# Fused FFT convolution and Mish MLP on one Trainium2 core: h's octet transform moved directly in front of kv's

## The chip, the cores and the metric

The kernel runs on one core of a Trainium2 chip. A core has five engines with a queue of their own each: TensorE (PE, matrix products, with its weight loads listed as PEld), VectorE (DVE), ScalarE (ACT), GpSimd (POOL) and SyncE (SP, which here only issues DMAs). Each engine works its queue off in order, and an instruction that waits for another engine's count (a semaphore) holds up all that stands behind it. Products land in PSUM, from where ScalarE or VectorE must copy them out. The metric is the device time of one execution in microseconds; lower is better.

## The reference, cut to what matters

With S = 2048 positions, D = 448 channels, F = 1792:

```python
xn = _layernorm(A_q)
# A: an H3 block
k_shift = sum_t k_pad[:, t:t + S, :] * shift_k[:, ks - 1 - t]     # causal, 4 taps
kv = k_shift * v
y = irfft(rfft(kv, 2 * S) * rfft(ssm_k, 2 * S))[:, :S] + kv * ssm_D
A = xn * y
# B: an MLP
h = xn @ w1 + b1
B = (h * tanh(softplus(h))) @ w2
return A_q + A + B
```

All of it is float32. The long convolution is done by a transform in stages, written as small matrix products.

## The kernel before, in words

The MLP is the spine. It is cut into 8 chunks of 256 positions (`NCHUNK`), and each chunk into 7 pairs of 128 columns of F (`NP`), 56 pairs in all. A pair takes two **slots** (half steps) on TensorE: an even slot with its first product (`g1_mm`, line 494, 22 matrix products), an odd slot with the Mish of this pair on ScalarE (`mish`, line 502, with a cast `ach` and on VectorE the remainder `acl`, line 81) and the second product of the pair two before (`g2_mm`, lines 519 to 521, 12 products). Float32 is made of a high and a low part, so each product is done three times.

The convolution is laid between these slots by a plan of numbers: `at(slot, fn)` puts a piece ahead of the slot's MLP work, `after(slot, fn)` behind it. First come the transforms over 64 points (`f1_mm`, for the filter "h" and for "kv"); their results go to DRAM. From slot 63 on come eight **octets** o. For each:

- `o_load` (lines 195 to 201): SyncE loads the octet's part of h's and of kv's first transform, tiles "ah" and "av" (one buffer each), and the matrices "g"; `gi_load` loads "gi" for the way back.
- `h2_mm` and `v2_mm` (line 214): the second transform, 16 products each into two PSUM tiles "pc". The trace lists each as two instructions, so a block is 32. They use a quarter of the array each, 64 rows by 32 columns.
- `h2_out` and `v2_out` (lines 225 and 234): the copies from PSUM to the tiles "hs" and "vs".
- `prod` (line 247): the complex product of the two on VectorE, in two parts of three instructions: part 0 makes "ya" (with "yb"), part 1 "yc" (with "yd"). The four tiles have one buffer each.
- `i1_mm` (line 257): the first step of the way back, from "ya" and "yc" into two tiles "pc"; `i1_out` (line 265) copies them out and stores them to the DRAM tile "E".

The pool "pc" has two tiles in all, of two PSUM banks each. Octet o has its kv block in slot s = 65 + 3 o and its inverse in slot s + 4, one slot after the kv block of octet o + 1. So three slots hold, in turn, kv of o, the inverse of o - 1, and h of o + 1. Between these VectorE also normalises the inputs of chunks 5 to 7 (`nt_norm`, line 434, tiles "xn", and `nt_split`, line 442, "XL"), takes their statistics (line 389), and adds the MLP's result (`g2_evac`, line 526, tile "qt"). Small VectorE pieces are put between the larger ones by `dv()`.

After the octets, from slot 98, the last step of the way back follows (`i2_mm`, `gate`), and then the end of the MLP.

Of the kernel before, what the change touches and what calls it, by code (L numbers as in the profile page):

```python
# [14 lines left out]
S, D, F = 2048, 448, 1792  # L15
# [13 lines left out]
H0_AT = 63  # L29
# [10 lines left out]
def tile_kernel(ctx: ExitStack, tc, q, qT, k, v, sk, hT, sD, w10, w1, b1, w2, c_f1, c_id, c_g, c_gi, c_i2, out):  # L40
    nc = tc.nc
    V = nc.vector
# [14 lines left out]
    Dh = dp.tile([NO * 16, 32, D], F32, name="Dh")  # L57
# [39 lines left out]
    def at(slot, fn, *args):  # L97
        plan.setdefault(int(slot), []).append((fn, args))

    def after(slot, fn, *args):  # L100
        plan2.setdefault(int(slot), []).append((fn, args))
# [85 lines left out]
    GT, AH, AV, HS, PV, Y = {}, {}, {}, {}, {}, {}  # L187

    def t2(shape, name, bufs=1):
        if not sp2:  # L190
            ph1.close()
            sp2.append(ph2.enter_context(tc.tile_pool(name="ph2", bufs=1, reuse_waits="tile")))
        return sp2[0].tile(shape, F32, name=name, bufs=bufs)
# [28 lines left out]
    def h2_out(o):  # L222
        HS[o] = t2([128, 2, 2, D], "hs", 2)
        for c, p in enumerate(PS.pop(("H", o))):
            nc.scalar.copy(HS[o][:, c], p[:, :, :D])  # L225

    def v2_mm(o):
        PS["V", o] = [f2_mm(AV[o], o, c) for c in range(2)]
# [353 lines left out]
    for g, t in enumerate(KV_AT):  # L582
        d = t - (KV_AT[g - 1] if g else t - 6)
# [17 lines left out]

    for o in range(NO):
        s, d = OCT_AT[0] + OCT_AT[1] * o, OCT_AT[1]
        h = s - 1 if o else H0_AT
        (at if o else after)(h - d if o else h - 4, o_load, AH, Dh, o, "ah")
        at(s - d if o else s - 2, o_load, AV, Dkv, o, "av")
        at(h, h2_mm, o)
        after(h, h2_out, o)
        at(s, v2_mm, o)
        after(s, v2_out, o)  # L610
        at(s, gi_load, o)
        after(s + 1, prod, o, 0)
        after(s + 2, prod, o, 1)
        at(s + 4, i1_mm, o)
        after(s + 4, i1_out, o)

# [84 lines left out]
    for s in range(nslots):  # L701
        j = s // 2 - G2_LAG - 1
        if s % 2 == 0 and j >= 0 and pairs[j][1] == NP - 1:
            g2_evac(pairs[j][0])
        for fn, args in plan.pop(s, ()):
            fn(*args)
        mlp_slot(s)
        fns = plan2.pop(s, ())
        for fn, args in fns:
            if fn in (h2_out, v2_out, i1_out):  # L710
                fn(*args)
        for fn, args in fns:
            if fn not in (h2_out, v2_out, i1_out):
                fn(*args)
# [66 lines left out]
```

## Time and profile before

| | |
|---|---|
| median of 3 runs | 365.48 us (365.23 to 365.75) |
| profiled execution, its time | 365.54 us |
| its span | 363.8 us |
| mean granted clock of TensorE | 0.998 |
| busy: TensorE, VectorE, ScalarE | 98%, 74%, 46% of the span |
| the octets (h of octet 0 to the inverse of octet 7) | 182.0 to 293.5 us of the span |

The span is the time between the first and the last instruction of the profile; the rest of the execution's time lies around it. In the timeline a row gives start, duration, engine, line, operation, tiles (out<-in) and, in brackets, the idle time ahead of it and what ended it. In the chain of work a row gives start, duration, engine, tile and line.

### The profile page before, as it was taken

Reading aid. Unit: us, or ns where it says so; the run is one execution under the profiler, and the core shown is the slowest. Engines: PE = TensorE matmul, PEld = TensorE weight load, DVE = VectorE, ACT = ScalarE, POOL = GpSimd, SP = SyncE. Lnnn points to the kernel's source line nnn. Section 1 sums busy time; section 2 is a strip of 40 time slices with the busy share of each in tenths; the row PEclk is TensorE's granted clock in tenths of the full one; section 3 lists DMA queues with packets and bytes.
Section 4 is the critical chain, followed back from the end, with each engine's and each line's share of the span. In section 5 each row is a group of like instructions: output and inputs, shape, how many; then the busy total and the mean of one; then the engine's idle time right before and its main releaser. Section 6 shows DMA issues by size and latency. Waiting matters only on the chain.

```text
span 363.8 us, 7474 instructions
## 1 busy us (share of the span) xinstructions
PE 357.8 (98%) x3110; PEld 290.1 (80%) x3110; DVE 267.4 (74%) x367; ACT 166.4 (46%) x279; POOL 74.3 (20%) x67
## 2 busy tenths in 40 slices
PE   8999999999999999999999999999999999999995
PEld 2988888888888989988967666666666889889885
DVE  5798658999998988797427755767665734997741
ACT  4866552344333433343255555547655534225450
POOL 3027002931028223604000020000010005112020
PEclk9999999999999999999999999999999999999999
DMA  7999978758686438525877798898898486959656
GB/s 251 353 270 349 413 300 231 225 158 264 154 264 199 92 121 268 146 70 119 235 261 217 258 245 218 290 272 219 266 271 189 90 253 235 406 221 278 108 68 135
DMA packets 32515, 81.69 MB, mean 225 GB/s; under 512 B 3025, under 2 KB 19026, under 8 KB 32482
## 3 DMA queue, kind: packets, MB, share of 16 engines
q1 hardware_dynamic: 21266, 47.16, 39.1%
q10 hardware_dynamic: 8240, 19.34, 21.6%
q0 software_dynamic: 2976, 14.73, 13.8%
q8 instruction: 24, 0.39, 0.4%
q14 instruction: 9, 0.07, 0.1%
HBM read 52.77 MB, written 28.45 MB: 223 GB/s over the span
## 4 chain that ended last, share of the span: by engine, by line
PE 54%; DVE 2%; ACT 1%; ACTq 1%; issue 0%
PE pg L494 20%; PE pg L519 7%; PE pc L214 7%; PE pg L521 7%; PE pg L520 7%; PE pc L257 4%; PE pc L314 2%; ACTq L268 1%; DVE x L178 1%; PE pc L131 1%; DVE x L181 0%; ACT qe L265 0%; ACT a L502 0%; ACT hs L225 0%; DVE qt L526 0%
## 5 line engine op out<-in xcount | busy, mean ns | idle before, releaser
L502 ACT ACTIVATE a<-pg,b1t 128x256 f32<-128x256 f32 x112 | 47.2, 473 | 109.1 <-PE pg L494 95.8
L494 PE MATMUL pg<-XH,w1h 128*128 128x256 f32 x448 | 90.8, 285 | 0.4 <-DVE XL L457 0.2
L494 PEld LDWEIGHTS pg<-XH,w1h 128*128 128x128 f32 x448 | 69.7, 188 | 18.7 <-issue 16.5
L519 PE MATMUL pg<-w2h,ach 128*128 128x448 f32 x224 | 83.2, 371 | 0.0
L520 PE MATMUL pg<-w2l,ach 128*128 128x448 f32 x224 | 81.3, 363 | 0.2 <-DVE w2l L81 0.2
L521 PE MATMUL pg<-w2h,acl 128*128 128x448 f32 x224 | 81.4, 363 | 0.0
L81 DVE TENSOR_TENSOR acl<-a,ach 128x512 fp32r<-128x512 f32 x56 | 38.7, 691 | 57.5 <-ACT ach L80 57.4
L494 PE MATMUL pg<-XL,w1h 128*128 128x256 f32 x448 | 69.7, 277 | 0.0
L494 PEld LDWEIGHTS pg<-XL,w1h 128*128 128x128 f32 x448 | 59.5, 188 | 0.0
L494 PE MATMUL pg<-XH,w1l 128*128 128x256 f32 x336 | 56.8, 278 | 0.0
L519 PEld LDWEIGHTS pg<-w2h,ach 128*128 128x128 f32 x224 | 42.0, 187 | 14.4 <-issue 12.2
L494 PEld LDWEIGHTS pg<-XH,w1l 128*128 128x128 f32 x336 | 46.9, 188 | 0.0
L520 PEld LDWEIGHTS pg<-w2l,ach 128*128 128x128 f32 x224 | 42.1, 188 | 2.8 <-DVE w2l L81 0.5
L521 PEld LDWEIGHTS pg<-w2h,acl 128*128 128x128 f32 x224 | 42.1, 188 | 2.6
L80 ACT CAST ach<-a 128x512 fp32r<-128x512 f32 x56 | 34.7, 620 | 1.8
L161 POOL TENSOR_TENSOR x<-kr,skb 128x896 f32<-128x896 f32 x8 | 17.0, 2126 | 74.5 <-DVE x L160 53.2
L178 DVE TENSOR_TENSOR x<-x 128x896 f32<-128x896 f32 x24 | 26.3, 1097 | 2.7 <-POOL x L161 2.2
L398 POOL TENSOR_TENSOR mv<-ve,mhalf 128x2 f32<-128x2 f32 x3 | 3.7, 1248 | 97.9 <-DVE ve L395 97.9
L402 POOL TENSOR_SCALAR xn<-qt,mv,rstd 128x448 f32<-128x448 f32 x8 | 21.8, 2720 | 0.4
L137 ACT COPY st<-pc 128x896 f32<-128x896 f32 x16 | 14.5, 906 | 14.5 <-PE pc L131 12.6
L138 DVE TENSOR_TENSOR st<-pc,st 128x896 f32<-128x896 f32 x16 | 17.4, 1088 | 4.5 <-ACT st L137 4.1
L265 ACT COPY qe<-pc 128x896 f32<-128x896 f32 x16 | 13.8, 911 | 12.0 <-PE pc L257 11.8
(85 smaller groups left out, 404.1 us busy)
## 6 DMA issues: line engine op xcount, KB each, us to landing
Dkv<-st ACTq DMA_DIRECT2D x16, 448.0 KB, 6.2
ah<-Dh SPq DMA_DIRECT2D x8, 896.0 KB, 7.4
av<-Dkv SPq DMA_DIRECT2D x8, 896.0 KB, 6.3
E<-qe ACTq DMA_DIRECT2D x16, 448.0 KB, 5.7
e<-E POOLq DMA_DIRECT2D x8, 896.0 KB, 8.0
kr<-in_k_dram SPq DMA_DIRECT2D x10, 448.0 KB, 6.5
Dh<-st ACTq DMA_DIRECT2D x10, 448.0 KB, 5.7
x<-in_hT_dram SPq DMA_DIRECT2D x8, 448.0 KB, 6.9
```

The source lines that it names most:

```text
L80: nc.scalar.copy(h, raw)
L81: V.tensor_sub(l, raw, h)
L138: V.tensor_add(st[:, 0], e, st[:, 1])
L161: nc.gpsimd.tensor_mul(o, KR[g - u // 2], skb[:, u:u + 1].to_broadcast([128, 2, D]))
L178: V.tensor_add(KV[g], KV[g], o)
L214: nc.tensor.matmul(p[32 * t:32 * t + 32, r, :D], g[rs, t, c], a[rs, t], start=True, stop=True, tile_position=(64 * r, 32 * t))
L402: eng.tensor_scalar(xn[:, jj, :D], Q[c][:, jj], mv[:, j, 0:1], rs(c)[:, jj:jj + 1], op0=ALU.subtract, op1=ALU.mult)
L494: nc.tensor.matmul(ps[n], l, r, start=all(m[0] != n for m in seq[:n_]), stop=all(m[0] != n for m in seq[n_ + 1:]))
L502: nc.scalar.activation(a[:, n], ps[n], AF.Mish, bias=b1t[:, 2 * p + n:2 * p + n + 1])
L519: nc.tensor.matmul(ps, ah[:, n, cs], w2h[:, f], start=f == 0, stop=False)
L520: nc.tensor.matmul(ps, ah[:, n, cs], w2l[:, f], start=False, stop=False)
L521: nc.tensor.matmul(ps, al[:, n, cs], w2h[:, f], start=False, stop=f == NF - 1)
```

## The change

Three things change for each octet. `h2_mm` stands in slot s with `v2_mm`, directly in front of it; before it stood one slot earlier (octet 0: in slot 63, two slots earlier). The copy of h's PSUM tiles is no longer two ScalarE instructions of 896 columns but four of 448, one of each pair on ScalarE and one on VectorE; they are issued directly behind h's block (`at` in place of `after`). And both parts of `prod` are issued one slot sooner, in s and s + 1. The load of "ah" follows `h2_mm` of the octet before, so it moves with it; for octet 0 it stays in slot 59.

```diff
     def h2_out(o):
         HS[o] = t2([128, 2, 2, D], "hs", 2)
         for c, p in enumerate(PS.pop(("H", o))):
-            nc.scalar.copy(HS[o][:, c], p[:, :, :D])
+            nc.scalar.copy(HS[o][:, c, 0], p[:, 0, :D])
+            V.tensor_copy(HS[o][:, c, 1], p[:, 1, :D])
...
     for o in range(NO):
         s, d = OCT_AT[0] + OCT_AT[1] * o, OCT_AT[1]
-        h = s - 1 if o else H0_AT
-        (at if o else after)(h - d if o else h - 4, o_load, AH, Dh, o, "ah")
+        (at if o else after)(s - d if o else H0_AT - 4, o_load, AH, Dh, o, "ah")
         at(s - d if o else s - 2, o_load, AV, Dkv, o, "av")
-        at(h, h2_mm, o)
-        after(h, h2_out, o)
+        at(s, h2_mm, o)
+        at(s, h2_out, o)
         at(s, v2_mm, o)
         after(s, v2_out, o)
         at(s, gi_load, o)
-        after(s + 1, prod, o, 0)
-        after(s + 2, prod, o, 1)
+        after(s, prod, o, 0)
+        after(s + 1, prod, o, 1)
```

One line is added in `h2_out`, so all line numbers between it and the octets' plan are one higher in the changed kernel.

On TensorE, slots 82 and 83 (octet 6, tiles "ah" and "av") stand like this before; what a first row waits for is in brackets, DMAHW being a DMA's count and the other names those of engines:

```order
L214 MATMUL pc<-ah,g 32x448 [waits DMAHW6_49,DMAHW1_49,Activation_49]
L214 MATMUL pc<-ah,g 32x448 x7
L214 MATMUL pc<-ah,g 32x448 [waits Activation_49]
...
L494 MATMUL pg_3060<-XL,w1h 128x256 x4
L214 MATMUL pc<-av,g 32x448 [waits DMAHW4_49,Activation_49]
L214 MATMUL pc<-av,g 32x448 x7
L214 MATMUL pc<-av,g 32x448 [waits Activation_49]
```

And after:

```order
L495 MATMUL pg_3053<-XL,w1h 128x256 x4
L214 MATMUL pc<-ah,g 32x448 [waits DMAHW3_49,DMAHW2_49,Activation_49]
L214 MATMUL pc<-ah,g 32x448 x7
L214 MATMUL pc<-ah,g 32x448 [waits Activation_49]
L214 MATMUL pc<-av,g 32x448 [waits DMAHW4_49,DVE_49]
L214 MATMUL pc<-av,g 32x448 x7
L214 MATMUL pc<-av,g 32x448 [waits DVE_49]
L520 MATMUL pg_2719<-w2h,ach 128x448
```

h's block has moved behind the first product of slot 82, directly in front of kv's, and kv's two halves now wait for VectorE's count where they waited for ScalarE's.

On VectorE, the products of octet 5 and what lies among them stand like this before:

```order
L434 TENSOR_TENSOR xn<-xn,idr 128x4x128 [waits DVE_49]
L81 TENSOR_TENSOR acl<-a,ach 128x512 [waits PE_49,Activation_49]
L247 TENSOR_TENSOR ya<-vs,hs 128x896 [waits PE_49]
L247 TENSOR_TENSOR yb<-vs,hs 128x896
L247 TENSOR_TENSOR ya<-ya,yb 128x896 [waits DVE_49]
L442 TENSOR_TENSOR XL<-xn,XH 128x4x128 [waits Activation_49]
L247 TENSOR_TENSOR yc<-vs,hs 128x896 [waits PE_49]
L389 BN_STATS bst<-qt 128x6 [waits DMAHW2_49]
L247 TENSOR_TENSOR yd<-vs,hs 128x896
```

And after:

```order
L248 TENSOR_TENSOR ya<-ya,yb 128x896 [waits DVE_49]
L435 TENSOR_TENSOR xn<-xn,idr 128x4x128 [waits DMAHW6_49]
L435 TENSOR_TENSOR xn<-xn,idr 128x4x128 [waits DVE_49]
L81 TENSOR_TENSOR acl<-a,ach 128x512 [waits Activation_49]
L248 TENSOR_TENSOR yc<-vs,hs 128x896 [waits PE_49]
L248 TENSOR_TENSOR yd<-vs,hs 128x896
L248 TENSOR_TENSOR yc<-yc,yd 128x896 [waits DVE_49]
L443 TENSOR_TENSOR XL<-xn,XH 128x4x128 [waits Activation_49]
L226 COPY hs<-pc 128x448 [waits Activation_49] x2
```

The products have moved ahead of the input's normalisation, and behind all of it stand the two new copies of octet 6. They wait for ScalarE's count alone; in the built program it is the count that ScalarE's own copy of the same tile raises.

## The prediction

> **What bounds the kernel now.** I read the page's first part, then PE's waits, then the chain that ended last.
>
> ```profile
> span 363.8 us, 7474 instructions
> PE 357.8 (98%) x3110; PEld 290.1 (80%) x3110; DVE 267.4 (74%) x367; ACT 166.4 (46%) x279; POOL 74.3 (20%) x67
> ...
> PE pg L651 <- DVE wz L647: 1.0, 1, 1.0
> ...
> PE pc L214 <- ACT hs L225: 0.2, 1, 0.2
> ```
>
> TensorE is busy for 98% of the span, and inside the octets it waited once, 0.2 us. So the kernel is as long as TensorE's queue: whatever shortens a block of that queue is won, and every wait put into it is lost in full, since nothing later has slack to give it back. The question is what a block costs and whether the new order makes TensorE wait. The chain gives the blocks (start, us, what):
>
> ```profile
> 170.96 0.94 PE pc L131 x16
> 171.90 0.40 PE pg L519
> ...
> 226.15 1.79 PE pc L214 x32
> ...
> 243.62 1.69 PE pc L257 x32
> 245.31 2.69 PE pg L494 x22
> ...
> 248.00 1.67 PE pc L214 x32
> 249.67 0.40 PE pg L519
> 250.07 0.20 PE pg L520
> ...
> 252.28 1.66 PE pc L214 x32
> 253.94 2.71 PE pg L494 x22
> ...
> 286.94 2.51 PE pg L494 x22
> ...
> 291.85 1.69 PE pc L257 x32
> ```
>
> A transform block (L214: h or kv; L257: the inverse) works on slices of the array, the MLP's halves (L494 is the first product, "g1"; L519 to L521 the second, "g2") on all of it. Sixteen instructions take 0.94, thirty-two 1.66: sixteen alone are 0.72, and **entering** such a block costs 0.94 - 0.72 = 0.22. **Leaving** it costs the next half 0.20: its first L519 takes 0.40 instead of 0.20, and g1 takes 2.71 instead of 2.51. A g2 half is 2.61 behind a block (249.67 to 252.28) and 2.40 without (289.45, where g1 ended, to 291.85).
>
> **What the change saves.** h's and kv's blocks become one. That saves one entry and one exit, 0.42 per octet, 3.4 over eight, if kv's block can start when h's ends. In the kernel before, an octet pays 1.66 + 0.20 + 1.66 + 0.20 = 3.72 for both.
>
> **What it adds: kv needs h's PSUM.** The pool "pc" has two buffers. h's block fills both, so kv's first half (c=0) waits until h's c=0 tile has been copied out; before, a whole MLP half lay between them and hid this. The copy is now two instructions, and in the built program VectorE's does not wait for TensorE: it waits for ScalarE's count at its own copy of the same tile. The halves go one after the other, not side by side. Their prices:
>
> ```profile
> L225 ACT COPY hs<-pc 128x896 f32<-128x896 f32 x16 | 13.7, 908 | 3.7 <-PE pc L214 3.7
> ...
> L459 ACT CAST XH<-pg 128x512 fp32r<-128x512 f32 x9 | 5.3, 587 | 17.0 <-PE pg L447 16.9
> ...
> L459 ACT CAST XH<-pg 128x256 fp32r<-128x256 f32 x2 | 0.6, 376 | 0.5 <-PE pg L447 0.5
> ...
> L526 DVE TENSOR_TENSOR qt<-pg,qt 128x448 f32<-128x448 f32 x16 | 9.3, 618 | 4.4 <-PE pg L521 4.4
> ...
> L402 DVE TENSOR_SCALAR xn<-qt,mv,rstd 128x448 f32<-128x448 f32 x2 | 1.0, 508 | 0.4 <-POOL rstd L398 0.4
> ...
> 230.70 0.84 ACT L502 ACTIVATE a<-pg,b1t 128x256 f32<-128x256 f32 x2 [0.87 <-PE pg L494]
> 231.57 0.62 ACT L80 CAST ach<-a 128x512 fp32r<-128x512 f32 x1
> ...
> 232.22 0.69 DVE L81 TENSOR_TENSOR acl<-a,ach 128x512 fp32r<-128x512 f32 x1 [2.01 <-ACT ach L80]
> 232.83 1.09 DVE L247 TENSOR_TENSOR ya<-vs,hs 128x896 f32<-128x896 f32 x1
> ...
> 235.96 1.08 DVE L247 TENSOR_TENSOR yc<-vs,hs 128x896 f32<-128x896 f32 x1
> ...
> 253.30 1.72 ACT L234 COPY vs<-pc 128x896 f32<-128x896 f32 x2 [1.28 <-PE pc L214]
> ```
>
> ScalarE for 448 columns out of PSUM: between 376 ns (256) and 587 (512), 0.53. VectorE's 448-column copy has no row; the ends are 0.51 (L402, no PSUM) and 0.62 (L526, which reads PSUM, so I take it). The Trainium skill ("VectorE: DVE Perf Modes", the section on the TRN2 errata) gives a PSUM source 120 + 448 cycles at 0.96 GHz, 0.59 as an estimate; with it the sum would be 0.2 lower. A follower starts 0.03 after the one it waits for (cast ends 232.19, acl starts 232.22).
>
> From the start of h's block: c=0 is ready at 1.02 (252.28 to 253.30); ScalarE copies until 1.55; VectorE from 1.58 until 2.20; kv may start at 2.23, while h ends at 1.66. TensorE waits 0.57. What kv then costs lies between 1.44 (twice 0.72, as if nothing had stopped) and 1.79 (the block at 226.15 that followed a wait); I take an ordinary block, 1.66. The c=1 tile is ready at 1.74, copied by 2.92, and kv's c=1 comes at 2.23 + 0.94 = 3.17: no wait. So kv ends at 3.89, with the exit 4.09: **0.37 more than 3.72 per octet, 3.0 over eight** (ends 0.0 and 0.5, so 0.3 to 4.1).
>
> **VectorE's queue in front of those copies.** This is the larger term. The copies stand in order behind all of the previous octet's products. Those products cannot start earlier by being issued earlier: part 0 of octet o overwrites "ya", which the inverse block of octet o-1 reads, and this block still comes one slot later.
>
> ```profile
> 206.50 0.62 DVE L389 BATCH_NORM_STATS2 bst<-qt 128x6 f32<-128x448 f32 x1
> 207.04 1.07 DVE L247 TENSOR_TENSOR ya<-vs,hs 128x896 f32<-128x896 f32 x1
> ...
> 241.51 1.41 DVE L434 TENSOR_TENSOR xn<-xn,idr 128x512 f32<-128x512 f32 x2
> 244.73 1.09 DVE L247 TENSOR_TENSOR ya<-vs,hs 128x896 f32<-128x896 f32 x1 [1.81 <-PE pc L257]
> ...
> 262.08 0.69 DVE L442 TENSOR_TENSOR XL<-xn,XH 128x512 fp32r<-128x512 f32 x1
> 262.69 1.09 DVE L247 TENSOR_TENSOR yc<-vs,hs 128x896 f32<-128x896 f32 x1
> ...
> 287.95 1.15 DVE L526 TENSOR_TENSOR qt<-pg,qt 128x448 f32<-128x448 f32 x2
> 289.01 1.08 DVE L247 TENSOR_TENSOR yc<-vs,hs 128x896 f32<-128x896 f32 x1
> ```
>
> ya starts 1.11 after its inverse block does (243.62, 244.73). From that block's start, h of octet o+1 comes after 1.69 + 2.71 + 2.40 = 6.80 (the other parity: 1.69 + 2.61 + 2.51, the same), and VectorE's copy is due 1.58 later, at 8.38. So VectorE has 8.38 - 1.11 = **7.27 us** for all that stands between. Start to start: three products 3.13 (232.83 to 235.96), six 6.26; acl 0.61; XL 0.61; a BN_STATS 0.54; the pair of xn 1.41; the pair of qt 1.06. BN_AGGR and its like are left out. Late by octet:
>
> - copies of octet 1: no inverse yet; ya waits for ScalarE's first kv copy, at 4.67 (hs until 1.74 + 0.53 = 2.27, a Mish pair and its cast 1.49, from 230.70 to 232.19, the copy 0.91); then 6.26 + XL + acl + xn = 8.89, to 13.56; due at 3.89 + 2.61 + 2.51 + 2.40 + 1.58 = 12.99: 0.6.
> - octet 2: two BN_STATS, XL and acl, 8.56. XL now stands behind ya's three products and g1 of slot 70 needs it: it ends at 1.11 + 3.13 + 1.08 + 0.69 = 6.0, TensorE asks at 1.69 + 2.61 + 7/22 of 2.51 = 5.1: a wait of 0.9. The copies are then late by 8.56 - 7.27 - 0.9 = 0.4.
> - octet 3: acl and qt, 7.93: 0.7. Octet 4: acl, 6.87: in time, by 0.4.
> - octets 5 and 6: xn, XL, acl, 8.89: 1.6 each. Octet 7: one BN_STATS and acl, 7.41: 0.1.
>
> Together 0.6 + 1.3 + 0.7 + 0 + 1.6 + 1.6 + 0.1 = **5.9**. Each wait delays the next inverse equally, so it neither builds up nor heals. If VectorE were 0.3 sooner in each octet it would be 4.3, if 0.3 later 7.7; 0.3 is about what my leaving out of small rows and of half of a wait can make.
>
> **What costs nothing.**
>
> ```profile
> 245.35 1.72 ACT L265 COPY qe<-pc 128x896 f32<-128x896 f32 x2 [2.86 <-PE pc L257]
> 247.10 1.25 ACTq L268 DMA_DIRECT2D E<-qe  x2
> ...
> ah<-Dh SPq DMA_DIRECT2D x8, 896.0 KB, 7.4
> av<-Dkv SPq DMA_DIRECT2D x8, 896.0 KB, 6.3
> ```
>
> ScalarE loses eight times 2 x (0.91 - 0.53) and has slack: it has issued E's stores 4.73 after the inverse began (243.62 to 248.35), a Mish pair and cast end near 6.2, and the hs copy is due at 7.8. The Mish behind the copies is needed four slots later. On SyncE's queue gi moves ahead of g, ah and av; it waits for an inverse long done. ah is issued when h is done, av when kv is, as before; each still has some 11 us to its next use against 7.4 and 6.3. What is new is that the two start 2.2 us apart instead of 4.4. Octet 0's h moves from slot 63 to 65 in front of kv, its load stays in slot 59.
>
> **Sum.** +3.0 + 5.9 = +8.9 on the profiled execution's 365.54 (the median of the runs is 365.48, 0.06 less): **374.4**.
>
> **Rivals.**
> - *The change pays.* VectorE comes in time and both halves are out by 1.66: then the whole 0.42 x 8 = 3.4 is won, 362.1. It decides at 0.64 from ready to free (1.02 to 1.66); one copy behind the other takes 0.53 + 0.62 and two followers' starts, 1.21, before any lateness. The Trainium skill says under "TensorEngine Tiling (Array Packing)", PSUM Bottleneck, to empty PSUM with ScalarE and VectorE both; by that rule this is the outcome, and the trace has no pair of copies that ran side by side from one tile to bear it out. Chance 0.06.
> - *Only the chain of two copies costs.* VectorE's queue is ahead of my count and just the 0.3 to 4.1 remain: 365.8 to 369.6. For it: VectorE is idle a quarter of the span. Against: that idle time lies ahead of ya and acl, where it waits for TensorE and ScalarE (1.81 and 2.01 in the rows above), so it cannot be spent on the products. Chance 0.11.
> - *The loads collide.* If ah and av shared the DMA evenly and both took 7.4 + 6.3 = 13.7 from h's end at 1.66, ah would land at 15.4 and h, due at 3.89 + 2.61 + 6.80 = 13.3, wait 2.1 in seven octets: 14.7 more, 389. Against: ah starts first, and it moves no more bytes per octet than before. Chance 0.05.
> - *My forecast*, VectorE late: 0.78.
>
> The forecast's own ends are 0.3 + 4.3 = 4.6 and 4.1 + 7.7 = 11.8 more, 370.1 to 377.3; the range reaches a little past them, below into the second case: 369.0 to 378.0. Under 0.2% (0.7 us) a measurement here tells nothing from no change; of the second case some falls there: faster 0.06, same 0.02, slower 0.92.
>
> **What would show it.** In PE's waits, L214 for VectorE's hs copy at the new line, 9 to 11 us in all, the longest ahead of kv of octets 5 and 6; one wait of g1 for XL near 1 us. In the chain, products and hs copies of VectorE ahead of kv. h to kv's end 3.9 where VectorE is in time (octet 4). g halves without a block in front at 2.40 and 2.51. ya waiting for L257's successor in seven octets instead of three. I am wrong if kv's block follows h's with no wait, or if the first wait there ends with a DMA.

## The result, and the profile after

The changed kernel takes **379.69 us** (median of 6 runs, 377.73 to 380.13) against 365.62 (6 runs, 365.23 to 366.07) beside it: 1.037 times as long, with an interval of 1.0353 to 1.0388. That is 14.1 us more where 8.9 were forecast, and it lies above the range of 369.0 to 378.0. The profiled execution took 380.13, its mean granted clock was 0.991. The runs follow that clock in part: three at 0.991 took 379.58 to 380.13, the one at 0.999 took 377.92, just inside the range.

The page's first part for the changed kernel, and TensorE's waits (engine, line, whom it waited for: us in total, times, longest):

```profile
span 378.3 us, 7495 instructions
PE 361.1 (95%) x3110; PEld 292.1 (77%) x3110; DVE 275.7 (73%) x383; ACT 161.8 (43%) x279; POOL 76.2 (20%) x67
```

```profile
PE pc L214 <- DVE hs L226: 9.2, 8, 2.1
PE pg L520 <- DVE qt L527: 1.8, 1, 1.8
...
PE pg L495 <- DVE XL L443: 0.9, 1, 0.9
```

TensorE has the same 3110 matrix instructions as before, now stands still for some 12 us in the octets, and is also 3.3 us longer busy (361.1 against 357.8). The waits of 9.2 for the hs copies and 0.9 for XL are what was forecast (9 to 11, and near 1); the one for qt and the longer busy time were not forecast.

The chain that ended last, around octets 4, 5 and 6 and at the MLP's result behind octet 7 (start, us, what):

```profile
241.33 1.00 PE pc L214 x16
...
242.35 0.54 ACT hs L225
...
242.91 0.64 DVE hs L226
...
243.59 1.74 PE pc L214 x32
245.33 0.40 PE pg L520
...
257.92 0.55 DVE hs L226
258.51 2.62 PE pc L214 x32
261.12 3.50 PE pg L495 x22
...
275.19 2.27 PE pc L214 x32
...
303.16 0.55 DVE qt L527
```

In octet 4 nothing is late: h's first half, ScalarE's copy, VectorE's copy, kv, one after the other, 4.00 from h's start to the end of kv (241.33 to 245.33). In octets 5 and 6 VectorE's copies come later, and there kv's block itself takes 2.62 and 2.27 instead of 1.74, and the first product behind octet 5's takes 3.50 instead of 2.71.

VectorE's timeline shows why the copies of octet 5 are late, and what stands ahead of qt:

```profile
249.03 1.09 DVE L248 TENSOR_TENSOR ya<-vs,hs 128x896 f32<-128x896 f32 x1 [3.29 <-PE pc L258]
...
256.63 0.68 DVE L443 TENSOR_TENSOR XL<-xn,XH 128x512 fp32r<-128x512 f32 x1
257.23 0.68 DVE L81 TENSOR_TENSOR acl<-a,ach 128x512 fp32r<-128x512 f32 x1
257.83 1.15 DVE L226 COPY hs<-pc 128x448 f32<-128x448 f32 x2
...
302.07 1.09 DVE L248 TENSOR_TENSOR yc<-yc,yd 128x896 f32<-128x896 f32 x1
303.08 1.15 DVE L527 TENSOR_TENSOR qt<-pg,qt 128x448 f32<-128x448 f32 x2
```

VectorE is idle for 3.29 until the inverse block lets it overwrite ya, and then works without a pause until the hs copies at 257.83. At the end, qt starts where the last product of octet 7 ends.

The windows give the clock: window, its length, busy time of PE, PEld, DVE, ACT and POOL (with counts), then the granted TensorE clock, the DMA share and GB/s. They are laid where the clock changes.

```profile
255.82:259.23 3.41, 1.31 (x32) 0.34 (x24) 3.16 (x5) 1.00 (x2) 0.00 (x0) 1.00 0.97 274
259.23:262.64 3.41, 3.41 (x31) 1.86 (x16) 0.00 (x0) 1.81 (x2) 0.00 (x0) 0.50 0.95 302
...
272.88:276.29 3.41, 1.39 (x32) 0.50 (x32) 3.38 (x6) 2.08 (x6) 0.00 (x0) 1.00 0.66 187
276.29:279.71 3.42, 3.42 (x22) 2.12 (x7) 0.52 (x1) 1.81 (x2) 0.00 (x0) 0.50 0.59 175
...
300.19:303.60 3.41, 1.72 (x16) 1.52 (x14) 3.38 (x4) 1.46 (x3) 0.00 (x0) 1.00 0.98 219
303.60:307.01 3.41, 3.26 (x28) 2.58 (x36) 1.22 (x3) 0.00 (x0) 0.00 (x0) 1.00 0.49 172
```

TensorE waits 2.1 and 2.0 us, and shortly after it works again its clock is 0.50 for 3.41 us, both times. Behind the wait of 1.8 for qt it stays at 1.00. What decides this is taken up at e8_stalls.

**Where the 14.6 us of the profiled execution went** (380.13 against 365.54):

- The chain of two copies: octet 4's 4.00 and an exit of 0.20 make 4.20, where the two blocks cost 3.72 before: 0.48 in each of eight octets, 3.8.
- VectorE late in front of the hs copies: octet 4's wait is 0.60 (from h's end, 1.66 after 241.33, to 243.59), eight of these are 4.8, and 9.2 was waited: 4.4. XL 0.9 more.
- qt: 1.8.
- The clock: kv and g1 of octet 5 0.88 and 0.79 above 1.74 and 2.71; kv of octet 6 0.53, and the g2 half behind it about 1.1 above its 2.61: 3.3. Half of twice 3.41 is 3.4, so the two ways of counting agree.

Together 14.2; 0.4 is spread too thinly to place. No wait of TensorE in the octets ends with a DMA.

### The profile page after: what moved, and what is told of

It is laid out like the page before. It is cut to its first block, busy times and chain, and to the rows that moved or that the text cites. A ratio compares the mean times of both kernels' runs of the same rounds, so it can differ in the third digit from the quotient of the medians.

```text
span 378.3 us, 7495 instructions
## 1 busy us (share of the span) xinstructions
PE 361.1 (95%) x3110; PEld 292.1 (77%) x3110; DVE 275.7 (73%) x383; ACT 161.8 (43%) x279; POOL 76.2 (20%) x67
## 4 chain that ended last, share of the span: by engine, by line
PE 39%; DVE 16%; issue 4%; ACT 1%; DVEq 0%
PE pg L495 15%; PE pg L520 5%; PE pg L522 5%; PE pg L521 5%; PE pc L214 4%; DVE yc L248 4%; PE pc L258 2%; DVE yb L248 2%; DVE ya L248 2%; DVE yd L248 2%; PE pc L315 2%; DVE acl L81 1%; DVE xn L435 1%; DVE hs L226 1%; DVE XL L443 1%
## 5 line engine op out<-in xcount | busy, mean ns | idle before, releaser
L248 DVE TENSOR_TENSOR ya<-vs,hs 128x896 f32<-128x896 f32 x8 | 8.7, 1092 | 34.2 <-PE pc L258 28.6
L399 POOL TENSOR_TENSOR mv<-ve,mhalf 128x2 f32<-128x2 f32 x3 | 5.5, 1841 | 115.0 <-DVE ve L396 115.0
L214 PE MATMUL pc<-av,g 64*32 64x448 f32 x256 | 15.3, 588 | 9.2 <-DVE hs L226 9.2
```

The costliest lines, as they stand in the source:

```text
L214: nc.tensor.matmul(p[32 * t:32 * t + 32, r, :D], g[rs, t, c], a[rs, t], start=True, stop=True, tile_position=(64 * r, 32 * t))
L248: f(*x)
```

## The experiments

Theories: the forecast's account (called A where an expectation gives letters) is a chain of two copies plus a VectorE queue that is late because ya has one buffer. Its rivals: that two blocks directly behind one another on two PSUM tiles cost this much, whoever copies (B); that the sooner products themselves are what makes the copies late (C); and that the clock's fall has another cause than the length of the wait ahead of it (D). No experiment leaves work of the reference out; e8_stalls adds work.

### e1_scalar_copies and e2_move_only: without VectorE's copies, and then without the sooner products

e1 is the changed kernel with h's PSUM copied by ScalarE alone:

```diff
-            nc.scalar.copy(HS[o][:, c, 0], p[:, 0, :D])
-            V.tensor_copy(HS[o][:, c, 1], p[:, 1, :D])
+            nc.scalar.copy(HS[o][:, c], p[:, :, :D])
```

e2 also puts the products back into their old slots, so that only the move of h's block is left:

```diff
-        after(s, prod, o, 0)
-        after(s + 1, prod, o, 1)
+        after(s + 1, prod, o, 0)
+        after(s + 2, prod, o, 1)
```

> The changed kernel, but h's PSUM is copied by ScalarE alone, two copies of 896 columns as before. Theory A (VectorE's queue): kv waits only for ScalarE's first copy, 1.02 + 0.91 + 0.04 = 1.97 after h's start, some 0.4 per octet with the restart, and no octet is late; XL's wait of about 1.2 and qt's of about 2 stay, since the products are still early; the granted clock stays at 1.00. Sum 8 x 0.4 - 1.6 for the exits + 1.2 + 2.0 - 0.3: 370 us. Theory B (the adjacency itself: two PSUM tiles for two blocks, whoever copies): kv's waits stay near 9 us in all, 376 us or more.

> As the run with ScalarE's copies, and the products issued in their old slots, so that of the change only h's move in front of kv is left. Theory A: the waits for XL and qt go too, since XL and qt stand ahead of the products again; kv waits 0.4 per octet, less 0.2 per octet for the saved exit: 367 us, 1 to 2 above before. Theory B: 373 us or more.

Measured: e1 370.6 (1.0143 of the kernel before, 1.0126 to 1.0159); e2 367.61 (1.0059, 1.0044 to 1.0074). TensorE's waits in e1:

```profile
PE pc L214 <- ACT hs L225: 2.6, 8, 0.4
```

Both as expected, and B falls: with ScalarE's copies kv waits 2.6 in all, not some 9. One ScalarE copy of 896 columns (0.91) makes kv wait 0.3 per octet, at most 0.4; the pair split over two engines made it wait 0.60 at best and 2.1 at worst. e1 still waits 1.9 for qt and 0.9 for XL; in e2 both waits are gone, and so are 3.0 us: the sooner products cost just that and bring nothing when VectorE has no copies to make. The move alone is 2.2 us slower than the kernel before.

### e3_products_back: the split copies with the products in their old slots

The edit is e2's second one alone.

> The changed kernel with the two-engine copies kept and only the products back in their old slots. Theory A: the products start no later, because ya waits for the inverse either way, so kv's waits stay near 9 to 10 us with the two long ones near 2 us and the clock's drop behind them; only the waits for XL and qt (3 us) go: 376 to 377 us. Theory C (the products' new place makes VectorE late): kv's waits fall to 5 us, 0.6 per octet, 369 to 370 us.

Measured: 389.51 (1.0668, 1.0629 to 1.0707), clock 0.976. All values given were too low. TensorE's waits, and VectorE's timeline ahead of one octet's copies:

```profile
PE pc L214 <- DVE hs L226: 16.6, 8, 3.3
```

```profile
230.66 0.69 DVE L81 TENSOR_TENSOR acl<-a,ach 128x512 fp32r<-128x512 f32 x1 [1.98 <-ACT ach L80]
...
235.47 1.14 DVE L226 COPY hs<-pc 128x448 f32<-128x448 f32 x2
```

With the products later, acl comes between their two parts and VectorE stands still for 1.98 until ScalarE has cast; yc, qt and the copies all come that much later. So with split copies the sooner products are a help (of 9.8 us), not the cause of the lateness: C falls. Part of the 9.8 is the clock, which stood at 0.50 behind five of these waits, of 2.24 to 3.32 us, where the changed kernel has two such spells. What I had not counted is that a queue's delay depends on who else's work its instructions wait for, not only on their number.

### e4_ya_two: ya in two buffers

Part 0 of the products no longer has to wait for the inverse; to make room, yd shares yb's buffer.

```diff
-            Y[o] = a, c, b, e = [t2([128, 2, D], n) for n in ("ya", "yc", "yb", "yd")]
+            a, c, b = t2([128, 2, D], "ya", 2), t2([128, 2, D], "yc"), t2([128, 2, D], "yb")
+            Y[o] = a, c, b, b
```

> The changed kernel with two buffers for ya, so that part 0 of the products does not wait for the inverse block of the octet before (yd shares yb's buffer to make room; same instructions). Theory A: VectorE gains 3 us per octet, the copies are in time everywhere, kv waits only for the chain of two copies, 0.67 per octet; no waits for XL and qt, no drop of the clock: 8 x 0.67 - 1.6 - 0.3 = 3.5 more than before, 369 us. Theory B: 376 us or more, since the order of blocks and copies is the same.

Measured: 369.49 (1.0113, 1.0094 to 1.0132), clock 1.00.

```profile
PE pc L214 <- DVE hs L226: 5.0, 8, 0.8
```

As expected. The waits fall to 0.6 per octet, those for XL and qt disappear, and so does the low clock. This takes out the forecast's second term: one buffer of ya costs 10.2 of the 14.1 us, in lateness, in XL and qt, and in the clock that the longest waits bring down. What is left, 4.0 over the kernel before, is the chain of two copies (3.8 above).

### e7_norm_first: products last among a slot's pieces

In the changed kernel, the pieces that follow a slot's MLP work are issued with the products behind the others:

```diff
-        for fn, args in fns:
-            if fn not in (h2_out, v2_out, i1_out):
-                fn(*args)
+        rest = [(fn, args) for fn, args in fns if fn not in (h2_out, v2_out, i1_out)]
+        for fn, args in sorted(rest, key=lambda f: f[0] is prod):
+            fn(*args)
```

> The changed kernel, but among the pieces of one slot the products come last, so that xn and XL of the input's normalisation fill the time in which ya waits for the inverse. Theory A: VectorE is 1.4 sooner for the copies of octets 5 and 6; their waits of 2.1 and 2.0 fall to about 0.7, and the half-rate clock behind them goes with them (3.3 us); XL of slot 70 comes in time (1.2): 373 us, and the granted clock is 1.00 throughout. Theory D (the clock's drop has another cause than the length of the wait): the drops stay, 376 us or more.

Measured: 378.87 (1.0356, 1.0328 to 1.0383): g1's wait for XL is gone, but the sum of the hs waits is 9.8 instead of 9.2. In VectorE's timeline ahead of octet 5's copies:

```profile
253.01 0.69 DVE L443 TENSOR_TENSOR XL<-xn,XH 128x512 fp32r<-128x512 f32 x1 [1.14 <-ACT XH L442]
```

A gain to 373 did not come. XL now stands between the products' parts and waits 1.14 for ScalarE's cast, so the copies, at 257.35, are as late as before. The reason is that of e3 again. Octet 6 gains (its wait is 1.38 instead of 2.02), and octet 1, where XL waits for its cast ahead of ya, loses more (2.08 instead of 0.78). The waits did not become short, so this run alone does not decide about D.

### e8_stalls: waits of six lengths put into the kernel before

Behind the octets, in slots 93 to 111, TensorE is made to wait for chains of 1 to 8 small VectorE additions, each between two extra products of 128 columns.

```diff
+STALLS = ((93, 1), (96, 3), (100, 4), (103, 5), (107, 6), (111, 8))
...
+        nc.tensor.matmul(p[:, 0, :128], wq, wq, start=True, stop=True)
+        V.tensor_copy(sq, p[:, 0, :128])
+        for _ in range(n):
+            V.tensor_add(sq, sq, sq)
+        nc.tensor.matmul(p[:, 1, :128], sq, wq, start=True, stop=True)
```

> The kernel before with six waits put into TensorE's queue at slots 93, 96, 100, 103, 107 and 111: a small product, a VectorE copy of it and a chain of 1, 3, 4, 5, 6 and 8 small additions on it, and a product that reads the result; waits of about 0.9 to 3.5 us. It measures the clock by itself. Theory A: behind the waits under 1.9 us the clock stays 1.00 and the next halves take 2.4 to 2.7; behind those of 2.0 and more it is 0.50 for some 3.4 us and the halves there take 1.6 us more together. Theory D: the clock stays 1.00 behind all of them.

Measured: 396.21 in its one run, clock 0.978. Other VectorE work came between the additions, so the waits became 0.71, 3.59, 6.01, 2.01, 2.34 and 3.00 in this order. Two of them:

```profile
349.65 0.49 PE L656 MATMUL pc<-wq,sq 128*128 128x128 f32 x2 [2.01 <-DVE sq L655]
...
366.01 0.49 PE L656 MATMUL pc<-wq,sq 128*128 128x128 f32 x2 [2.34 <-DVE sq L655]
```

The wait of 2.01 was followed by half clock and the longer one of 2.34 was not, against the expectation under A. The waits of 3.00 and more all were, that of 0.71 was not. In e7 the waits of 2.08 and 2.02 ahead of kv of octets 1 and 5 were not, and the shorter one of 1.84 for qt was. So the length alone does not decide, and D, as e7's expectation has it, is right in this; that the clock would stay at 1.00 behind all waits of e8 is not.

The traces show what does. In all 14 of them the time between two changes of the granted clock is a whole multiple of 3.41 us: in e8 the clock falls at 316.58, 333.64, 350.71 and 381.43, which is 5, 5 and 9 times 3.41 apart, and in the changed kernel at 259.23 and 276.29, 5 times. So each execution can be cut into stretches of 3.41 us at whose borders the clock changes. Four such stretches, each with the one behind it, two of e8 and then two of e7:

```profile
347.29:350.71 3.42, 1.41 (x10) 1.17 (x9) 3.03 (x10) 1.46 (x3) 0.01 (x1) 1.00 0.94 361
350.71:354.12 3.41, 3.41 (x12) 3.02 (x11) 2.77 (x4) 1.26 (x2) 0.88 (x1) 0.50 1.10 231
...
364.36:367.77 3.41, 1.76 (x10) 1.67 (x11) 3.27 (x9) 1.20 (x2) 0.00 (x0) 1.00 0.66 120
367.77:371.19 3.42, 3.42 (x28) 3.36 (x27) 2.06 (x2) 0.68 (x2) 0.85 (x1) 1.00 0.39 31
```

```profile
198.25:201.66 3.41, 1.62 (x32) 0.38 (x30) 3.34 (x6) 1.06 (x2) 0.00 (x0) 1.00 0.24 26
201.66:205.08 3.42, 3.13 (x44) 1.96 (x45) 0.77 (x2) 2.04 (x3) 0.00 (x0) 1.00 0.75 262
...
297.23:300.64 3.41, 1.57 (x9) 1.27 (x9) 3.08 (x5) 1.46 (x3) 0.00 (x0) 1.00 0.65 165
300.64:304.06 3.42, 3.42 (x23) 2.18 (x29) 0.00 (x0) 0.00 (x0) 0.00 (x0) 0.50 0.39 140
```

TensorE's busy time is the first number behind the length. The wait of 2.34 lay across a border: 0.69 of standing still came into one stretch and 1.65 into the next, and the clock stayed. The wait of 2.01 lay in one stretch whole, and the next stretch had half clock. Over all 14 traces, from the first such border to the last of TensorE's work, 15 stretches at full clock have 1.84 us or more of standing still by the profile's busy time, and half clock follows each; in all others it is 1.79 or less (the stretch from 198.25 above), and half clock follows none. The 1.84 for qt lay in one stretch in e7 and e11, and half clock followed; in the changed kernel 0.15 of it lay ahead of a border, and none did. Where the borders lie differs from execution to execution, which fits the different mean clocks of the changed kernel's own runs (0.991 to 0.999); only the profiled one's borders are on record.

### e9_banks and e10_banks_before: two copies that really run side by side

The built program lets VectorE's copy wait for ScalarE's because both read one tile. Here each tile "pc" of two PSUM banks is cut into two of one bank, so that the copies have nothing in common; ya has two buffers as in e4. e10 cuts the tiles alike in the kernel before and changes nothing else.

```diff
-    pcp = pool("ps_c", 2, space=PSUM)
+    pcp = pool("ps_c", 4, space=PSUM)
...
-        return pcp.tile([128, 2, 512], F32, name="pc")
+        return [pcp.tile([128, 512], F32, name="pc") for _ in range(2)]
...
-            nc.scalar.copy(HS[o][:, c, 0], p[:, 0, :D])
-            V.tensor_copy(HS[o][:, c, 1], p[:, 1, :D])
+            nc.scalar.copy(HS[o][:, c, 0], p[0][:, :D])
+            V.tensor_copy(HS[o][:, c, 1], p[1][:, :D])
```

> A try at a better version: the changed kernel with ya in two buffers (yd shares yb), and with each tile of the pool pc cut into two tiles of one bank, so that ScalarE's copy of one half and VectorE's of the other depend on TensorE alone and run side by side (other copies out of pc become twice as many of half the size). Theory A: both are out 0.62 after ready, kv starts at about 1.7, as h ends; kv's waits under 0.2 per octet, and the saved entries and exits (0.42) nearly all stay: 363 us. Theory B (two tiles for two blocks): kv still waits 0.5 and more per octet, 367 us or more.

> The control for the run with tiles of one bank: the kernel before with the pool pc cut the same way and all copies on ScalarE as before. Theory A: the smaller copies lie beside TensorE's other work: 365 to 366 us, no change that counts. If it is below 364, the gain of the other run is the tiles' and not the side-by-side copies'.

Measured: e9 367.93 (1.0069, 1.005 to 1.0088); e10 365.42 (0.9999, 0.9985 to 1.0014). The cut alone changes nothing, as expected. e9 came out 5 us above its expectation. Its chain (line numbers of the octets' code are three higher), and VectorE ahead of the first of these copies:

```profile
200.38 0.54 DVE hs L229
200.97 1.73 PE pc L217 x30
212.21 3.46 PE pc L217 x64
...
228.73 1.30 PE pc L217 x16
...
252.40 4.07 PE pc L217 x64
```

```profile
198.34 0.68 DVE L81 TENSOR_TENSOR acl<-a,ach 128x512 fp32r<-128x512 f32 x1
198.95 1.43 DVE L441 TENSOR_TENSOR xn<-xn,idr 128x512 f32<-128x512 f32 x2
200.30 1.15 DVE L229 COPY hs<-pc 128x448 f32<-128x448 f32 x2
```

The copies do run side by side: in octet 4 ScalarE's starts at 240.54 and VectorE's at 240.58, where in the changed kernel they start at 242.35 and 242.91. In five octets h and kv run without a wait, all 64 instructions in 3.46. In octets 1, 3 and 5 kv still waits: the copies are now due 0.5 sooner, right as their PSUM is ready, and xn, qt, or XL and acl stand ahead of them. And even an octet without a wait does not save what was forecast: 3.46 and an exit are 3.66 against 3.72, 0.06 and not 0.42. kv's block takes 1.80 of it, where 1.44 would be twice sixteen products without an entry.

### e11_banks_after: one-bank tiles, and ya in one buffer

The edit is e9's without that of ya.

> The changed kernel with every PSUM tile of the transforms cut into one-bank tiles, and ya still in one buffer. If the chain of two copies and VectorE's late queue are two separate costs, the chain's 0.57 in each of eight octets goes and the queue stays: 379.7 - 4.6 = 375, with L217 waits for DVE hs that are long only ahead of octets 2, 5 and 6. If they are one cost (the copies are late anyway, so it does not matter that they could run side by side), 378 or more. If the banks alone are what e9_banks gained, 368.

Measured: 376.98 (1.0312, 1.0291 to 1.0333), 2.7 under the changed kernel. TensorE's products waited 2.3 for the hs copies and 1.8 for qt; its weight loads waited longer:

```profile
PEld pc L217 <- DVE hs L229: 8.4, 11, 2.0
```

It falls between the two values given, 375 and 378. Where VectorE is in time (octets 0 and 4) most of the chain's 0.6 is won; where it is late, h to the end of kv takes about as long as before, or longer (octet 1: 4.72 against 4.18). Of the 2.1 between the two profiled executions (378.01 and 380.13) some 1.7 is the clock, which stood at 0.50 for one stretch here and for two there. So with a late queue the order of the two copies is worth little. With e4 and e9 the four cases are complete: neither 379.7, banks alone 377.0, ya alone 369.5, both 367.9. The second buffer of ya is worth 10.2 and 9.1, the one-bank tiles 2.7 and 1.6.

### e13_last_products: part 1 of octet 7's products behind qt

```diff
-        after(s + 1, prod, o, 1)
+        after(s + (2 if o == NO - 1 else 1), prod, o, 1)
```

> The changed kernel with the second part of octet 7's products alone back in slot 88, behind the qt adds. If those products ahead of qt cost what g2 waited, the wait of 1.8 goes: 377.9, and 376.4 where the low clock behind it goes too; the waits for hs stay as they are (9 to 10 in all). If the inverse of octet 7 then waits for yc instead, 379.7.

Measured: 377.25 (1.0298, 1.0272 to 1.0324), 2.4 under the changed kernel and between the first two values given. g2 no longer waits for qt, the waits for hs are as before, and the inverse does not wait in place of g2. VectorE's timeline:

```profile
300.15 1.15 DVE L527 TENSOR_TENSOR qt<-pg,qt 128x448 f32<-128x448 f32 x2
301.21 1.08 DVE L248 TENSOR_TENSOR yc<-vs,hs 128x896 f32<-128x896 f32 x1
```

qt starts at 300.15 where it started at 303.08. The edit moves nothing else, so the term that the forecast left out is shown. Its size is best read from the two profiled executions, which both have two stretches at half clock: 378.23 against 380.13, 1.9, for a wait of 1.8. The runs of this kernel also price the clock: the one with a mean clock of 1.00 took 374.96, the one with 0.99 took 378.23, 3.3 apart.

### e12_banks_order and e14_banks_cleared: VectorE's queue cleared ahead of the copies

Both are e9 with three pieces moved: qt of slot 74 behind octet 3's copies, xn of chunk 5's second half behind octet 1's (slot 68 for 67), XL of chunk 6's first half two slots later. e12 also issues products last in every slot, as e7; e14 only puts the normalisation first in slot 68.

```diff
-            after(b + NT_AT["norm"][jj], nt_norm, c, jj)
-            after(b + NT_AT["split"][jj], nt_split, c, jj)
+            after(b + NT_AT["norm"][jj] + (c == NT and jj == 1), nt_norm, c, jj)
+            after(b + NT_AT["split"][jj] + 2 * (c > NT and jj == 0), nt_split, c, jj)
...
-        if s % 2 == 0 and j >= 0 and pairs[j][1] == NP - 1:
+        evac = s % 2 == 0 and j >= 0 and pairs[j][1] == NP - 1
+        if evac and s < OCT_AT[0]:
             g2_evac(pairs[j][0])
         for fn, args in plan.pop(s, ()):
             fn(*args)
+        if evac and s >= OCT_AT[0]:
+            g2_evac(pairs[j][0])
```

> e9_banks with VectorE's queue cleared in front of the three late pairs of copies: qt of slot 74 behind octet 3's copies, xn of chunk 5's second half behind octet 1's, XL of chunk 6 behind octet 5's, products last among a slot's pieces. If only what stands ahead of the copies made kv of octets 1, 3 and 5 late (3.02, 3.12 and 2.41 against 1.67), 367.9 - 1.35 - 1.45 - 0.74 = 364.4, 1.0 under the kernel before, and every kv block at 1.7. If the block pair has another cost of its own, 366 to 368.

> e9_banks with VectorE's queue cleared in front of the three late pairs of copies, and the products left first among a slot's pieces: qt of slot 74 behind octet 3's copies, xn and XL of chunk 5's second half behind octet 1's, XL of chunk 6's first half two slots later. e12_banks_order, which put products last, made all but octets 1 and 6 run h and kv in 3.46 and lost there what it had won. If order in VectorE's queue is all that is left, every pair takes 3.46 to 3.5 and the time is 364.4 to 364.9, under the kernel before by 0.5 to 1.0. If something is late again elsewhere, 366 to 368, and a wait says what.

Measured: e12 367.85 (1.0066, 1.0052 to 1.0079), where 364.4 were expected if only the order counted: octets 3 and 5 are cleared, 1 is not, and 6 is late in their place, because XL now stands ahead of products again and waits for ScalarE. e14 **364.75** (median of 12 runs; 0.9978 of the kernel before, 0.9966 to 0.9989, beside 365.56 in 17 runs). Its chain, from octet 1 on:

```profile
198.72 3.46 PE pc L217 x64
...
263.36 3.46 PE pc L217 x64
...
276.22 4.13 PE pc L217 x64
```

and the reason for the one pair that is still longer, in VectorE's timeline:

```profile
277.33 0.69 DVE L81 TENSOR_TENSOR acl<-a,ach 128x512 fp32r<-128x512 f32 x1 [1.91 <-ACT ach L80]
277.94 1.15 DVE L229 COPY hs<-pc 128x448 f32<-128x448 f32 x2
```

The time is as expected: with VectorE's queue cleared in front of the copies the move is no longer a loss. The 0.8 us under the kernel before, 0.2%, are about the bound of what can be told here, and the trace does not show where they come from: its execution is the slowest of the twelve, 365.97, and there seven pairs win 0.06 each and the last one loses 0.6. Whether the pieces moved in VectorE's queue would win something in the kernel before, without the move, was not tried.

## Where the prediction was right and wrong

Right, by its own steps:

- *The sign and the mechanism.* kv waits for VectorE's copy, which waits for ScalarE's of the same tile and stands behind the products; e4 and e9 take the two causes apart.
- *kv needs h's PSUM.* +0.37 per octet was forecast, +0.48 measured: 0.03 more until kv starts (2.26 against 2.23), and 0.08 in kv's block (1.74, not 1.66). The two copies took what was put down for them, 0.53 and 0.62. As a term of the sum 3.8 for 3.0.
- *VectorE's queue in front of those copies.* 5.9 forecast; 4.4 and XL's 0.9 measured, with octet 4 in time and octets 5 and 6 the worst (0.60 + 1.5 and 0.60 + 1.4 for 0.57 + 1.6 each). Octet 1 was less late than forecast (0.2 for 0.6) and octet 7 more (0.45 for 0.1), which partly cancels in the sum.
- *What costs nothing*, for ScalarE, SyncE and the loads: none of them ends a wait in the octets.

Wrong, and why the time lies outside the range:

- *What stands behind octet 7's products was not looked at.* The step listed what stands between ya and the copies of the next octet, octet by octet, and so it ended with the copies of octet 7. Behind them part 1 of its products had moved ahead of qt, although a quoted row showed qt ahead of yc before. g2 waits 1.8 for it, and e13 shows it (1.9). The reading that gave XL's wait, what now stands ahead of an instruction that TensorE needs, would have given it in one line.
- *"Every wait put into it is lost in full"* was taken to mean its length. Two of the waits cost 1.6 us more each, since the clock was 0.50 for 3.41 us behind them: 3.3 that no term held. The prediction's rows of the kernel before, whose longest wait in the octets was 0.2, could not show it; but waits of 2.2 (0.57 + 1.6) were forecast without a word about the clock. That each of the two fell into one stretch is chance: in e7 waits of 2.08 and 2.02 lay across borders and cost nothing more. The trace differs here from the Trainium skill ("TensorE: Matmul & The Clock Gate", Part 1), which puts the fall to half rate behind an idle window of about 3.4 us: 1.84 us of standing still in a stretch were enough. That page also says that the window runs free of the program, and with this the traces agree (the borders 3.41 us apart at e8_stalls).
- *What the change saves.* The entry's 0.22 had been read from a block of another transform and shape (L131, 32 rows by 64 columns). 0.42 per octet with both copies in time, 3.4 in all, was the size of the rival "the change pays". e9 and e14 show 0.06 per octet (3.66 against 3.72), so even that rival would not have reached 362.1. What of kv's 1.80 is an entry paid again, and what a weight load held by a copy that comes just in time, is not separated: the cause of this part stays open.

The 8.9 forecast, 1.8 for qt, 3.3 for the clock and 0.8 for the longer chain, less 0.6 in the lateness, are 14.2 of the profile's 14.6. Neither of the two missing terms alone puts the forecast above 378.0 (374.4 + 1.8 = 376.2, 374.4 + 3.3 = 377.7); both together do. The rival "only the chain of two copies" is what e4 built, and there its 365.8 to 369.6 held (369.49). The Trainium skill's advice under "TensorEngine Tiling (Array Packing)", PSUM Bottleneck, to empty PSUM with both engines, did not hold in the changed kernel: from one shared tile and behind a late queue, both engines were 9.1 us slower than ScalarE alone (e1). With one-bank tiles and a cleared queue both engines took 364.75 (e14) against 367.61 for ScalarE alone (e2), but these two differ in more than the copies, so no run shows what the rule is worth there.

## What to carry to other kernels

Sharing a copy between two engines puts it into two queues: it ends when the later one gets to it, so read what stands ahead of it on both, and whether the built program orders the two reads of one tile. When work is moved sooner on a busy queue, list everything that it overtakes until the queue next runs empty, and for each piece whom it waits for and who waits for it. And price a wait of TensorE of some two us at up to 1.7 us more than its length: in these traces half clock follows for 3.41 us when 1.84 us or more of standing still fall into one stretch of 3.41 us; the same wait across a border between two stretches may go free, as e8's 2.34 did.

## What was unexpected in the hardware

- The clock's grid: half clock comes in whole stretches of 3.41 us, at borders that lie a multiple of 3.41 us apart within an execution. It followed each of 15 stretches in which TensorE stood still for 1.84 us or more, and none with 1.79 or less. A stretch costs up to 1.7 us.
- Two transform blocks directly behind one another take 3.46 (e9, e14), not 1.66 + 1.44: no entry is visibly saved, and only one exit's 0.20 less 0.14. Each of their products works on 64 rows by 32 columns, which is an eighth of the array's 128 by 128, not a quarter.
